# Segment sums of x added by accumulating DMAs in float32 instead of by matmuls, in a fused scan and memory-attention kernel

## The chip, the cores and the metric

The kernel runs on one core of one Trainium2 chip. The metric is device time in microseconds (us); lower is better. Each kernel was run several times. The engines are called as in the profile: PE is TensorE (matmuls), PEld its weight loads, DVE is VectorE, ACT is ScalarE, POOL is GpSimd, SP is SyncE.

## The reference, cut to what matters

The program computes two independent layers of the same width and joins their outputs. Layer A is a complex linear recurrence (a scan) over 2048 positions. Layer B is attention over 64 segments of 32 rows with an 8-row memory that is handed from segment to segment.

```python
# layer A
Bu = einsum('bld,pd->blp', x, B_bar)
for t in range(2048):
    h = Lam_bar * h + Bu[:, t, :]          # complex, 1024 states
y = 2 * einsum('blp,dp->bld', hseq, C).real + x * Dskip
# layer B, for each of 64 segments
h = concat([mem, xs])                      # 8 + 32 rows
o = softmax(mask(q k^T * scale)) v ; o = o @ Wo
mem = o[:, :8]                             # the next segment's memory
```

The kernel does not run layer B's 64 steps one after the other. It guesses every segment's memory from the mean of the segment's rows (the sum of 32 rows of x over L = 40, then through Wv and Wo), computes everything from the guess, and checks the guess at the end against a tolerance of 2^-8. If the check fails, a slow loop runs. The change concerns the segment sums that this guess starts from.

## The kernel before

In the "scan phase", about 35 to 347 us, TensorE works through a fixed list of steps. There are 32 scan blocks (block n = 4*pc + q) with 16 matmuls into the PSUM tile psU, and 32 "v groups" with four times 8 matmuls into psP. VectorE runs the scan of each block, and ScalarE copies both the scan's result (a_g) and the v results (b_vst) out of the way, in program order. This is part of a block:

```python
def stage1(self, pc, tb):
    u = k.ps("U", (128, 2, TB))                        # psU, 2 buffers
    ...  # 16 matmuls u <- a_xT, a_bt
    V.tensor_tensor(pr[:], u..., view(t3, ...), ALU.mult)   # the "large multiply"
    V.tensor_tensor(w, w, pr[:, :, 1, :], ALU.add)
    for j in range(2):
        V.tensor_tensor_scan(w[:, j, :], rb, w[:, j, :], carry, ALU.mult, ALU.add)
        S.activation(g[:, j, :], w[:, j, :], ACT.Copy)      # a_g, ScalarE
    ...  # the carry for the next block: five small instructions on GpSimd
    V.tensor_tensor(n[:], g..., view(r3, ...), ALU.mult)
    V.tensor_tensor(h[:], n[:, :, 0, :], n[:, :, 1, :], ALU.add)  # a_h
    k.SP.dma_start(self.hs[tb][:, pc, :, :], h[:])
```

The sums are made on TensorE, in eight groups of 16 matmuls that have only four columns each, one group ahead of each of the blocks 3 to 10:

```python
def sum_x(self, tmp):
    ...
    p = k.ps("R")
    for t in range(TT):                                # two t for each block
        xr = xrs.pop(t)                                # 128 rows of x, bf16
        for c in range(KC):
            o = c * NSEG + 4 * t
            k.PE.matmul(p[:, o:o + 4], xr[:, c * 128:(c + 1) * 128], k.ind[:], start=True, stop=True)
        load(t + 4)
        yield
    ...  # VectorE: xbar = p / L, with the memory's own mean in segment 0
```

The means are used by "og" groups (32 matmuls of 64 columns, psR<-b_xbar,b_wv), the first of which stood behind v group (3,3). Instructions that the program passes to `keep_in_program_order` are pinned within their engine; the others may be moved by the scheduler of the build.

Of the kernel before, what the change touches and what calls it, by code (L numbers as in the profile page):

```python
# [8 lines left out]
FP32 = mybir.dt.float32  # L9
BF16 = mybir.dt.bfloat16  # L10
I32 = mybir.dt.int32
ACT = mybir.ActivationFunctionType
ALU = mybir.AluOpType
# [26 lines left out]
EW = E + 8  # L40
# [53 lines left out]
def consts(k):  # L94
    nc, V, G = k.nc, k.V, k.G
    c = k.cst
    k.ident = c.tile([128, 128], BF16, name="ident")
    G.memset(k.ident[:], 1.0)
    G.affine_select(out=k.ident[:], in_=k.ident[:], compare_op=ALU.is_equal, fill=0.0, base=0,
                    pattern=[[-1, 128]], channel_multiplier=1)  # L100
    k.ones = c.tile([128, 1], BF16, name="ones")
    V.memset(k.ones[:], 1.0)
    k.hpb = c.tile([128, 1], FP32, name="hpb")
    k.hpe = c.tile([128, 1], FP32, name="hpe")
    V.memset(k.hpb[:], HALF_PI)
    k.S.activation(k.hpe[:], k.hpb[:], ACT.Exp)
    k.ind = c.tile([128, 4], BF16, name="ind")
    G.memset(k.ind[:], 0.0)
    for j in range(4):
        G.memset(k.ind[32 * j:32 * j + 32, j:j + 1], 1.0)  # L110


def masks(k):
# [223 lines left out]
class PartB:  # L337
# [34 lines left out]
        k.V.tensor_copy(self.memT[:, :, 0:NMX + 1], self.m0T[:])  # L372
        k.V.memset(self.accR[:], 0.0)

    def fill(self, tmp):
        k = self.k
        z = tmp.tile([32, 4 * EW], BF16, name="b_xr", bufs=4)
        k.V.memset(z[:], 0.0)
        for hb in range(HB):
            k.SP.dma_start(self.vx[hb][64 + NMX:GX, :], z[0:GX - 64 - NMX, :])  # L380
            k.SP.dma_start(self.vx[hb][T + 32:NSLOT, :], z[0:32, :])
        for q in range(4):
            k.SP.dma_start(self.tn[q][NM:NR, 0:4 * EW], z[0:NR - NM, :])
            k.SP.dma_start(self.tn[q][NM:NR, 1024 - 4 * EW:1024], z[0:NR - NM, :])
# [13 lines left out]
        return [(64 + 1536, 1536, 384), (0, XMAIN, 64), (T - 64, T - 64, 64)]  # L398

    def load_x0(self, tmp, i):  # L400
        self.x0.append(tmp.tile([128, D], BF16, name="b_xr", bufs=4))
        self.k.SP.dma_start(self.x0[i][:], self.x[0][64 + 128 * i:192 + 128 * i, :])

    def turn_x0(self, i):

        k = self.k
        pt = k.ps("U", (128, 2, KC, 128), BF16)[:, 0, :, :]
        for c in range(KC):
            k.PE.transpose(pt[:, c, :], self.x0[i][:, c * 128:(c + 1) * 128], k.ident[:])
        k.copy("vs"[i % 2], self.xe[:, :, 128 * i:128 * i + 128], pt)  # L410

    def sum_x(self, tmp):

        k = self.k
        xrs = {}

        def load(t):
            if t < TT:
                xrs[t] = tmp.tile([128, D], BF16, name="b_xr", bufs=4)
                k.SP.dma_start(xrs[t][:], self.x[0][t * 128:(t + 1) * 128, :])  # L420
        for t in range(4):
            load(t)
        yield
        p = k.ps("R")
        for t in range(TT):
            xr = xrs.pop(t)
            for c in range(KC):
                o = c * NSEG + 4 * t
                k.PE.matmul(p[:, o:o + 4], xr[:, c * 128:(c + 1) * 128], k.ind[:], start=True, stop=True)
            load(t + 4)  # L430
            yield
        pv = p[:].rearrange("p (c s) -> p c s", c=KC)
        ms = tmp.tile([128, KC], FP32, name="b_ms", bufs=1)
        k.V.tensor_reduce(ms[:], self.m0T[:], AX.X, ALU.add)
        k.V.tensor_scalar(self.xbar[:], pv, 1.0 / L, None, ALU.mult)
        k.V.tensor_tensor(ms[:], ms[:], pv[:, :, 0], ALU.add)
        k.V.tensor_scalar(self.xbar[:, :, 0], ms[:], 1.0 / L, None, ALU.mult)
        yield
# [536 lines left out]
def kernel_main(tc, A_x, A_Lre, A_Lim, A_Bre, A_Bim, A_Cre, A_Cim, A_logdt, A_Dskip, B_x, B_mem0, B_Wq, B_Wk, B_Wv, B_Wo, out,  # L975
                force=False, dbg=None):
    with ExitStack() as ctx:
        k = K(tc, ctx)
        k.dbg = dbg
        nc = k.nc  # L980
        a = PartA(k, A_x, A_Lre, A_Lim, A_Bre, A_Bim, A_Cre, A_Cim, A_logdt, A_Dskip, out)
        b = PartB(k, B_x, B_mem0, B_Wq, B_Wk, B_Wv, B_Wo, out)
# [11 lines left out]
        with pool("p1x", "right") as p1x, pool("p1", "right", 1) as p1:  # L994
            a.tab = a.tmp = a.wp = a.btp = p1
            k.pin |= {"PE", "SP"}
            warm(k, p1)
            w0 = b.wl.tile([128, KC, 512], BF16, name="b_wv", bufs=2)
            b.load_wv_part(w0, 0, 0, 128, nc.scalar)
            b.x0 = []  # L1000
            for i in range(4):
                b.load_x0(p1, i)
                if i in (1, 2):
                    b.load_wv_part(w0, 0, 128 * i, (256, 512)[i - 1])
            wv = {0: w0, 1: b.load_wv(1)}
            consts(k)
            a.load_params(p1)
            b.load_m0(p1)
            b.stage_init()
            order = steps()  # L1010
            b.v_x(0, 0, wv[0])
            b.load_x(1)
            a.load_b(0)
            a.xT = p1x.tile([128, KC, T], BF16, name="a_xT", bufs=1)
            a.load_x(0)
            a.params(p1, p1)
            b.init(p1)
            a.tables(0)
            loads = [[(b, 2)], [(a, 1), (a, 2)], [(b, 3), (a, 3)]]
            sx = b.sum_x(p1)  # L1020
            tabs = {0: a.tabs}
            bts = {0: a.bt}
            for kind, pc, q in order[1:]:
                if loads and kind == "v":
                    for o, n in loads.pop(0):
                        o.load_x(n)
                if kind == "v":
                    b.v_x(pc, q, wv[pc])
                    if q == 3:
                        if pc >= 3:  # L1030
                            b.og(pc, wv[pc])
                        n = (pc + 2) if pc + 2 < PC else (2, 0)[pc + 2 - PC]
                        wv[n] = b.load_wv(n)
                    continue
                a.tabs, a.bt = tabs[pc], bts[pc]
                n = 4 * pc + q
                if q == 2 and pc + 1 < PC:
                    a.load_b(pc + 1)
                    bts[pc + 1], a.bt = a.bt, bts[pc]
                if pc >= 4 and q == 1:  # L1040
                    a.load_c(pc - 4)
                if n == 1:
                    next(sx)
                if n >= 3:
                    for _ in range(2):
                        next(sx, None)
                a.stage1(pc, q)
                if q == 2 and pc + 1 < PC:
                    a.tables(pc + 1)
                    tabs[pc + 1] = a.tabs  # L1050
                if n == 12:
                    masks(k)
                    check_consts(k)
                if n == 14:
                    b.fill(p1)
            k.pin.remove("PE")
        psu.close()
        k.psx = ctx.enter_context(tc.tile_pool(name="pss", bufs=1, space=PSUM, reuse_waits="tile"))
# [5 lines left out]
        with pool("p2h", "right") as p2h, pool("p2", "right") as p2:  # L1064
# [5 lines left out]
            for i, _ in enumerate(s2):  # L1070
                if i in (1, 4, 7):
                    n = (2, 0, 1)[(i - 1) // 3]
# [148 lines left out]
```

## Time and profile before

| | before |
|---|---|
| time, median of the runs beside the change | 1247.47 us (1247.30 to 1248.05) |
| span of the profiled run | 1245.6 us |
| PE busy | 1234.4 us, 99% |
| chain that ended last | 98% PE |
| waits of PE of any size, 30 to 345 us | none |

The first lines are from the page of the kernel before: part 1, the busy time of each engine, and part 4, the chain of work that ended last, by engine.

```profile
PE 1234.4 (99%) x8270; PEld 662.3 (53%) x8342; DVE 668.0 (54%) x1250; ACT 263.5 (21%) x631; POOL 275.8 (22%) x407
...
PE 98%; DMA 1%; issue 0%; ACT 0%; POOL 0%; DVE 0%; SPq 0%; ACTq 0%
```

TensorE never stops. VectorE's 54% is an average over the whole program. The next lines are two of the 30 us windows of the same kernel, with the busy time of each engine, the granted clock, the DMA share and GB/s.

```profile
core 0: us, PE busy (x) PEld busy (x) DVE busy (x) ACT busy (x) POOL busy (x), PEclk, DMA share, GB/s
120.00:150.00 30.00, 29.84 (x166) 14.04 (x168) 26.56 (x28) 11.32 (x20) 9.96 (x15) 1.00 0.55 162
150.00:180.00 30.00, 29.84 (x166) 14.11 (x167) 29.05 (x27) 13.44 (x23) 7.97 (x10) 1.00 0.26 85
```

In the second window VectorE is busy for 29.05 of 30 us. The next lines are the timeline of PE in the kernel before; the columns are start, duration, engine, line, operation, tiles, shape and count.

```profile
60.13 7.07 PE L64 MATMUL psP<-b_wv,b_xe 128*128 128x512 bf16 x31
67.04 0.54 PE L64 MATMUL psR<-ind,b_xr 128*128 128x4 bf16 x16
67.44 3.61 PE L64 MATMUL psU<-a_xT,a_bt 128*128 128x512 bf16 x16
70.89 7.07 PE L64 MATMUL psP<-b_wv,b_xe 128*128 128x512 bf16 x31
```

One group of sum matmuls occupies 67.04 to 67.44, which is 0.40 us. Starts are to be subtracted, since the printed durations overlap. A scan block takes 3.45 us (70.89 less 67.44), so one 512-column matmul costs 0.216 us.

### The profile page before, as it was taken

How to read it: one execution, taken by the hardware profiler on the slowest of the kernel's cores; microseconds unless marked ns; L12 is line 12 of the kernel's file. 1: busy time of each engine (PE TensorE's matmuls, PEld its weight loads, DVE VectorE, ACT ScalarE, POOL GpSimd, SP SyncE). 2: the span in 40 equal slices, each digit the busy share in tenths (PEclk: the TensorE clock that was granted, in tenths of full speed). 3: DMA queues.
4: the chain of work that ended last, by engine and by line, in shares of the span. 5: the costliest groups of instructions: out<-in, count | busy, mean ns of one | idle time of the engine just before them, and what ended most of it. 6: DMA issues, size and time to landing. Idle time of an engine off the chain costs nothing.

```text
span 1245.6 us, 20120 instructions
## 1 busy us (share of the span) xinstructions
PE 1234.4 (99%) x8270; PEld 662.3 (53%) x8342; DVE 668.0 (54%) x1250; ACT 263.5 (21%) x631; POOL 275.8 (22%) x407
## 2 busy tenths in 40 slices
PE   9999999999999999999999999999999999999998
PEld 5444444444455555556666656555665554446444
DVE  4688899998711124666666666666666641001000
ACT  5344444443310000211112111111211110000000
POOL 4111331212332321322222222222222220000000
PEclk9999999999999999999999999999999999999999
DMA  9965444554898834664454544545473289407000
GB/s 245 272 192 148 131 132 128 144 156 107 241 323 247 251 116 95 192 167 123 95 144 108 144 108 114 138 92 133 96 155 95 61 223 220 110 18 153 17 17 27
DMA packets 316022, 176.83 MB, mean 142 GB/s; under 512 B 138650, under 2 KB 301326, under 8 KB 315926
## 3 DMA queue, kind: packets, MB, share of 16 engines
q1 hardware_dynamic: 293830, 147.95, 48.1%
q10 hardware_dynamic: 21072, 24.38, 5.9%
q0 software_dynamic: 1024, 3.17, 0.7%
q8 instruction: 66, 1.08, 0.4%
q14 instruction: 30, 0.25, 0.1%
HBM read 89.14 MB, written 53.17 MB: 114 GB/s over the span
## 4 chain that ended last, share of the span: by engine, by line
PE 98%; DMA 1%; issue 0%; ACT 0%; POOL 0%; DVE 0%; SPq 0%; ACTq 0%
PE psP L64 82%; PE psU L64 9%; PE psS L64 3%; PE psO L64 2%; PE psR L64 2%; DMA wo<-in_B_Wo_dram 1%; DMA b_xr<-in_B_x_dram 0%; ACT b_xe L89 0%; POOL b_m L644 0%; DVE b_ost L91 0%; SPq L64 0%; ACT b_e L641 0%; ACTq L89 0%
## 5 line engine op out<-in xcount | busy, mean ns | idle before, releaser
L64 PE MATMUL psP<-b_xe,b_wq 128*128 128x480 bf16 (+1 forms) x1280 | 247.7, 343 | 0.1
L64 PE MATMUL psP<-b_xe,b_wk 128*128 128x480 bf16 (+1 forms) x1280 | 247.7, 343 | 0.0
L64 PE MATMUL psP<-b_wv,b_xe 128*128 128x512 bf16 (+2 forms) x1033 | 223.4, 372 | 1.0 <-ACT b_xe L89 0.2
L644 POOL TENSOR_TENSOR b_m<-b_e,maskB 99x396 bf16<-99x396 bf16 x160 | 139.8, 874 | 334.0 <-ACT b_e L641 334.0
L641 ACT ACTIVATE b_e<-psS 99x396 bf16<-99x396 f32 x176 | 88.2, 501 | 532.2 <-PE psS L64 527.9
L64 PEld LDWEIGHTS <-b_wk 128*128 128x128 bf16 x1280 | 119.4, 98 | 94.2
L64 PEld LDWEIGHTS <-b_wq 128*128 128x128 bf16 x1280 | 118.7, 98 | 87.7
L64 PEld LDWEIGHTS <-b_xe 128*128 128x128 bf16 x1056 | 101.8, 98 | 119.1 <-ACT b_xe L89 0.4
L91 DVE CAST b_k<-psP 128x480 bf16<-128x480 f32 (+1 forms) x192 | 97.5, 529 | 101.1 <-PE psP L64 101.1
L91 DVE CAST b_q<-psP 128x480 bf16<-128x480 f32 (+1 forms) x192 | 97.5, 529 | 93.0 <-PE psP L64 91.4
L64 PEld LDWEIGHTS <-b_ol 128*128 128x128 bf16 x864 | 84.3, 98 | 94.4
L64 PE MATMUL psU<-a_xT,a_bt 128*128 128x512 bf16 x493 | 113.9, 379 | 1.1
L64 PE MATMUL psP<-t,a_hl 128*128 128x512 bf16 x496 | 112.1, 379 | 0.8
L91 DVE CAST b_ost<-psP 128x512 bf16<-128x512 f32 (+1 forms) x17 | 11.5, 676 | 183.4 <-PE psP L64 182.4
L64 PE MATMUL psP<-wo,b_ol 128*128 128x512 bf16 (+1 forms) x440 | 91.9, 364 | 0.4
L64 PE MATMUL psP<-t,b_ol 128*128 128x512 bf16 x408 | 91.7, 379 | 0.4
L280 POOL TENSOR_SCALAR a_tt<-a_pr,a_tabf 128x1 f32<-128x1 f32 x48 | 34.1, 709 | 243.5 <-DVE a_pr L275 243.5
L89 ACT ACTIVATE b_vst<-psP 128x512 bf16<-128x512 f32 x126 | 72.0, 589 | 71.0 <-PE psP L64 65.0
L661 DVE TENSOR_TENSOR b_ob<-psO,b_accR 99x384 bf16<-99x384 f32 x160 | 85.9, 553 | 2.0
L267 DVE TENSOR_TENSOR a_pr<-psU,a_tabf 128x2048 f32<-128x2048 f32 x32 | 73.0, 2282 | 15.7 <-PE psU L64 14.0
L64 PEld LDWEIGHTS <-a_bt 128*128 128x128 bf16 x512 | 49.2, 98 | 57.6
L64 PEld LDWEIGHTS <-a_hl 128*128 128x128 bf16 x512 | 49.1, 98 | 56.7
(200 smaller groups left out, 963.8 us busy)
## 6 DMA issues: line engine op xcount, KB each, us to landing
b_v<-b_vx SPq DMA_DIRECT2D x16, 1122.0 KB
b_wv<-in_B_Wv_dram SPq DMA_DIRECT2D x16, 1024.0 KB
b_on<-b_ob SPq DMA_DIRECT2D x15, 960.0 KB
b_vx<-b_vst ACTq DMA_DIRECT2D x24, 544.0 KB
a_hs<-a_h SPq DMA_DIRECT2D x32, 256.0 KB
b_wog<-in_B_Wo_dram SPq DMA_DIRECT2D x4, 2048.0 KB
b_wq<-in_B_Wq_dram SPq DMA_DIRECT2D x16, 512.0 KB
b_wk<-in_B_Wk_dram SPq DMA_DIRECT2D x16, 512.0 KB
```

Source lines behind the costliest of these rows:

```text
L64: r = f(*a, **kw)
L89: self.S.activation(out, in_, ACT.Copy)
L91: self.V.tensor_copy(out, in_)
L267: V.tensor_tensor(pr[:], u[:].unsqueeze(1).to_broadcast([128, 2, 2, TB]), view(t3, [[TB + 1, 2], [TB + 1, 2], [1, TB]]), ALU.mult)
L280: G.tensor_scalar(tt[:, j:j + 1], w[:, j, TB - 1:TB], t3[:, 1, TB:TB + 1], None, ALU.mult)
L641: k.S.activation(e[:], s[0:GW, :, :, 0:GW], ACT.Exp, scale=float(E) ** -0.5, accum_out=self.accE[0:GW, i:i + 1])
L644: k.G.tensor_tensor(m[0:GW, 0:4 * GP].rearrange("p (a b q) -> p a b q", a=2, b=2)[:, :, :, 0:GW], e[:], mask[0:GW, :, :].unsqueeze(2).to_b ...
L661: V.tensor_tensor(self.ob[:, b0:b0 + n, :], o[0:GW, 0:n, 0:E], r.unsqueeze(2).to_broadcast([GW, n, E]), ALU.mult)
```

## The change

The change wants the 3.2 us of sum matmuls off TensorE. Sixteen DMAs read x so that partition p gets row 16*p + j in the j-th DMA; the first two write float32 accumulators and fourteen add into them. VectorE adds the two accumulators (called the join below), ScalarE makes a bf16 high half, VectorE subtracts to get a low half, and 16 matmuls of 64 columns finish the sums, since now only two partitions belong to one segment. As the means are ready later, the first og group and one weight load move four blocks later.

```diff
-    def sum_x(self, tmp):
-        ...
-                xrs[t] = tmp.tile([128, D], BF16, name="b_xr", bufs=4)
-                k.SP.dma_start(xrs[t][:], self.x[0][t * 128:(t + 1) * 128, :])
-        ...
-                k.PE.matmul(p[:, o:o + 4], xr[:, c * 128:(c + 1) * 128], k.ind[:], start=True, stop=True)
+    def sum_x(self, tmp, ct):
+        k = self.k; G = k.G
+        acc = tmp.tile([128, 2, D], FP32, name="b_xr", bufs=1)
+        rows = self.x[0].rearrange("(p j) d -> p j d", j=16)
+        for j in range(16):
+            op = {"accum_op": ALU.add} if j > 1 else {}
+            k.tc.keep_in_program_order(G.dma_start(acc[:, j % 2, :], rows[:, j, :], **op))
+            if j % 2:
+                yield
+        s = acc[:, 0, :]
+        hl = ct[:, 0, 0:2, :]
+        k.tc.keep_in_program_order(k.V.tensor_tensor(s, s, acc[:, 1, :], ALU.add))
+        yield
+        k.tc.keep_in_program_order(k.S.activation(hl[:, 0, :], s, ACT.Copy))
+        yield
+        k.tc.keep_in_program_order(k.V.tensor_tensor(hl[:, 1, :], s, hl[:, 0, :], ALU.subtract))
+        yield
         yield
         p = k.ps("R")
+        for c in range(KC):
+            for i in range(2):
+                k.PE.matmul(p[:, c * NSEG:(c + 1) * NSEG], hl[:, i, c * 128:(c + 1) * 128], k.ind[:], start=(i == 0), stop=(i == 1))
@@ main loop
-                        if pc >= 3:
+                        if pc > 3:
                             b.og(pc, wv[pc])
                         n = (pc + 2) if pc + 2 < PC else (2, 0)[pc + 2 - PC]
-                        wv[n] = b.load_wv(n)
+                        if pc != 3:
+                            wv[n] = b.load_wv(n)
 ... (load_c of block n stands here, unchanged)
-                if n == 1:
-                    next(sx)
                 if n >= 3:
-                    for _ in range(2):
-                        next(sx, None)
+                    next(sx, None)
+                if n == 17:
+                    b.og(3, wv[3])
+                    wv[5] = b.load_wv(5)
                 a.stage1(pc, q)
```

Cut from the diff: `ind` becomes a 128x64 indicator built by two selects, the first four x tiles become slices of one tile, and a zero tile is taken from C's space.

More of the change, by code (lines that the diff above doesn't have):

```diff
@@ L106, in consts @@
     k.S.activation(k.hpe[:], k.hpb[:], ACT.Exp)
-    k.ind = c.tile([128, 4], BF16, name="ind")
-    G.memset(k.ind[:], 0.0)
-    for j in range(4):
-        G.memset(k.ind[32 * j:32 * j + 32, j:j + 1], 1.0)
+    k.ind = c.tile([128, NSEG], BF16, name="ind")
+    G.memset(k.ind[:], 1.0)
+    for base, m in ((0, 1), (1, -1)):
+        G.affine_select(out=k.ind[:], in_=k.ind[:], compare_op=ALU.is_ge, fill=0.0, base=base,
+                        pattern=[[-2 * m, NSEG]], channel_multiplier=m)
 def masks(k):
@@ L373, in init, with fill @@
         k.V.memset(self.accR[:], 0.0)
-    def fill(self, tmp):
+    def fill(self, ct):
         k = self.k
-        z = tmp.tile([32, 4 * EW], BF16, name="b_xr", bufs=4)
-        k.V.memset(z[:], 0.0)
+        z = ct[0:32, 0, 2, 0:4 * EW]
+        k.V.memset(z, 0.0)
         for hb in range(HB):
@@ L400, in load_x0 @@
     def load_x0(self, tmp, i):
-        self.x0.append(tmp.tile([128, D], BF16, name="b_xr", bufs=4))
-        self.k.SP.dma_start(self.x0[i][:], self.x[0][64 + 128 * i:192 + 128 * i, :])
+        if i == 0:
+            self.x0 = tmp.tile([128, 4, D], BF16, name="b_xr", bufs=1)
+        self.k.SP.dma_start(self.x0[:, i, :], self.x[0][64 + 128 * i:192 + 128 * i, :])
     def turn_x0(self, i):
@@ L408, in turn_x0 @@
         for c in range(KC):
-            k.PE.transpose(pt[:, c, :], self.x0[i][:, c * 128:(c + 1) * 128], k.ident[:])
+            k.PE.transpose(pt[:, c, :], self.x0[:, i, c * 128:(c + 1) * 128], k.ident[:])
         k.copy("vs"[i % 2], self.xe[:, :, 128 * i:128 * i + 128], pt)
-    def sum_x(self, tmp):
-        k = self.k
-        xrs = {}
-        def load(t):
-            if t < TT:
-                xrs[t] = tmp.tile([128, D], BF16, name="b_xr", bufs=4)
-                k.SP.dma_start(xrs[t][:], self.x[0][t * 128:(t + 1) * 128, :])
-        for t in range(4):
-            load(t)
+    def sum_x(self, tmp, ct):
[15 more added lines that the diff above has]
+        yield
         yield
         p = k.ps("R")
-        for t in range(TT):
-            xr = xrs.pop(t)
-            for c in range(KC):
-                o = c * NSEG + 4 * t
-                k.PE.matmul(p[:, o:o + 4], xr[:, c * 128:(c + 1) * 128], k.ind[:], start=True, stop=True)
-            load(t + 4)
-            yield
+        for c in range(KC):
+            for i in range(2):
+                k.PE.matmul(p[:, c * NSEG:(c + 1) * NSEG], hl[:, i, c * 128:(c + 1) * 128], k.ind[:], start=(i == 0), stop=(i == 1))
         pv = p[:].rearrange("p (c s) -> p c s", c=KC)
@@ L999, in kernel_main @@
             b.load_wv_part(w0, 0, 0, 128, nc.scalar)
-            b.x0 = []
             for i in range(4):
@@ L1019, in kernel_main @@
             loads = [[(b, 2)], [(a, 1), (a, 2)], [(b, 3), (a, 3)]]
-            sx = b.sum_x(p1)
+            sx = b.sum_x(p1, a.CT)
             tabs = {0: a.tabs}
@@ L1054, in kernel_main @@
                 if n == 14:
-                    b.fill(p1)
+                    b.fill(a.CT)
             k.pin.remove("PE")
```

## The prediction

> **What bounds the kernel.** TensorE: the page's first part has PE busy 1234.4 of 1245.6 us, and the chain of waits is 98% PE. The windows of 30 us between 30 and 330 us (scan phase, the only one the change touches) show PE at 29.8 of 30, DVE at 25 to 29. So only TensorE time counts, unless something new makes TensorE wait. VectorE is nearly co-critical there: from 150 to 287 us its large multiply (a_pr<-psU) waits for TensorE only twice, 1.8 us in all.
>
> **What is removed.** 128 segment-sum matmuls (psR<-ind,b_xr) in eight groups of 16, each before a scan block. In the timeline of PE a group starts at 67.04 and the next block's matmuls at 67.44: 0.40 us a group, all eight alike, 3.24 us in all. (The durations printed, 164 ns each, overlap and mislead.)
>
> **What is added.** 16 matmuls with 64 columns: the og group, same width, takes 0.93 us for 32 (170.39 to 171.32), so 0.47 us. Net TensorE gain 2.8 us. VectorE gets two fp32 128x1024 operations, 1.22 us each (as a_pr<-a_pr 128x1024 f32), ScalarE one copy of about 1.1 us. The xbar work and the first og copy only move.
>
> **The accumulating DMAs.** Sixteen 256 KB reads leave the SP queue for GpSimd's; 14 add into fp32. [...]the built order shows GpSimd waiting so, two chains of eight, in front of the scan carries. A plain 256 KB load from GpSimd lands in 5.8 us (DMA view); I estimate 6 to 9 us with the add. Carries are about 10 us apart and the fours fall in 20 us gaps, so I expect carries not to be late. The last pair is issued near 135 us, lands near 143; the VectorE join comes near 145 us. That margin is thin.
>
> **VectorE lag.** TensorE comes 2.8 us earlier, VectorE about 1 us earlier by block 16, so VectorE's lag grows by about 2 us. PSUM psU has two buffers; the smallest slack I find is 5.5 us: no stall.
>
> **The deferral.** og(3) and the wv load for pc 5 move from 170 to 195 us. In SP's order that load now follows the C transposes, which follow a_hs of block 16. Before, these issued at 208.4 to 214.4; now about 1 us earlier, so wv is issued near 213.4 and[...] lands near 219. TensorE wants it at 220.6-2.8 = 217.8. I expect a wait of about 1 us (0 to 3) on b_wv, which is new.
>
> **Sum.** 1247.49 - 3.24 + 0.47 + 1.0 + 0.3 (small ScalarE/psP waits) = 1246.0 us. Range 1243.8 to 1250.0. Chances: faster by over 2% 0.01, within 2% 0.96, slower by over 2% 0.03.
>
> **What would show it.** PE timeline: no gaps of 0.40 us before blocks 3 to 10, one of about 0.5 us before block 15, og (0.93 us) before block 17. Waits: PE or PEld waiting for DMA b_wv near 218 us, 0 to 3 us. GpSimd's timeline: carries start when VectorE's scan ends, not later. No VectorE wait for DMA b_xr at the join over 1 us. PE busy falls by about 3 us.
>
> **What would make it wrong.** Accumulating DMAs landing in over 10 us: GpSimd blocks, carries come late, VectorE, then ScalarE and psP evacuation, then TensorE stall, some us each block.[...] Or wv landing early: then 1244.7.

Three passages that no trace of this case shows are cut from this text, and the cuts are marked. The waits of GpSimd are waits for an earlier DMA into the same accumulator. The forecast's sum came to 1247.49 - 3.24 + 0.47 + 1.0 + 0.3 = 1246.0 us. Its 1.0 us is the wait on b_wv, 219 less 217.8 us, put at about 1; this term was the author's estimate. The trace after the change shows 1.04 us for ScalarE's copy, which the text puts at about 1.1.

## More of the kernel before

A v group takes four of psP's three rotating banks in turn, so its fourth set of 8 matmuls needs ScalarE's copy of an earlier one:

```python
    for i in range(4):
        p = k.ps("P")[:]                               # psP, 3 buffers
        self.v_mm(p, w, 4 * q + i)                     # 8 matmuls
        k.copy("s", st[:, i, :, 0:E], p...)            # b_vst, ScalarE
```

## The result, and the profile after

The changed kernel took 1258.87 us (1256.14, 1258.69, 1259.05 and 1259.61), against 1247.47 us before: 0.9% slower, and outside the predicted range. Ratios in this document are the mean time of one kernel's fast runs over the mean of the other's fast runs of the same rounds, so they are not quite the ratios of the medians quoted. Here the ratio is 1.0087, with a 95% interval of 1.0069 to 1.0104. The profiled run is the 1256.14 one (span 1254.4 us, 8.8 us more than before), and what follows explains these 8.8 us.

The page of the changed kernel, the same two parts as before:

```profile
PE 1234.1 (98%) x8159; PEld 659.2 (53%) x8230; DVE 670.0 (53%) x1252; ACT 264.6 (21%) x632; POOL 290.7 (23%) x421
...
PE 93%; DVE 3%; DMA 3%; issue 1%; POOL 0%; ACT 0%; SPq 0%; DVEq 0%; POOLq 0%
```

PE's busy time fell by only 0.3 us where 2.8 was expected, and its share of the chain fell from 98% to 93%, with DVE and DMA taking 3% each. The same two windows after the change:

```profile
120.00:150.00 30.00, 27.10 (x125) 12.22 (x125) 19.90 (x18) 8.31 (x15) 10.81 (x14) 1.00 0.75 211
150.00:180.00 30.00, 23.98 (x100) 10.41 (x102) 28.99 (x29) 13.68 (x23) 9.10 (x10) 0.89 0.18 66
```

VectorE lost 6.7 us in the first window; TensorE lost 2.7 us there and 5.9 us in the second, where its granted clock was also below 1. Every other window from 30 to 330 us has PE at 29.8 us. So the loss happens once. The timeline of DVE after the change shows where it starts; the bracket gives the idle time just before an instruction and what ended it. (Line numbers differ a little between kernels.)

```profile
136.79 0.69 DVE L288 TENSOR_TENSOR a_h<-a_n 128x1024 bf16<-128x1024 bf16 x1
146.64 1.23 DVE L427 TENSOR_TENSOR b_xr<-b_xr 128x1024 f32<-128x1024 f32 x1 [9.16 <-DMA b_xr<-in_B_x_dram]
147.78 2.28 DVE L268 TENSOR_TENSOR a_pr<-psU,a_tabf 128x2048 f32<-128x2048 f32 x1
```

VectorE finished block 9 at 137.5 us and came to the join, which stands ahead of block 10's large multiply (147.78) in its order. It waited 9.16 us for the last accumulating DMA, although psU for block 10 was full. The timeline of PE after the change shows the consequence:

```profile
143.59 3.62 PE L64 MATMUL psU<-a_xT,a_bt 128*128 128x512 bf16 x16
150.12 3.61 PE L64 MATMUL psU<-a_xT,a_bt 128*128 128x512 bf16 x16 [2.91 <-DVE a_pr L268]
153.57 5.34 PE L64 MATMUL psP<-b_wv,b_xe 128*128 128x512 bf16 x23
164.71 3.57 PE L64 MATMUL psP<-b_wv,b_xe 128*128 128x512 bf16 x8 [5.79 <-ACT b_vst L89]
168.07 4.01 PE L64 MATMUL psU<-a_xT,a_bt 128*128 128x512 bf16 x16
```

TensorE waits twice: 2.91 us for a psU buffer that VectorE had not read, and 5.79 us for a psP bank that ScalarE had not emptied. Then it is slow. The 8 matmuls from 164.71 take 3.36 us (to 168.07), 0.42 us each instead of 0.216. One-microsecond windows of the changed kernel, for PE alone, show why; PEclk, the number right after the count, is the granted clock as a share of full speed.

```profile
core 0: us, PE busy (x), PEclk, DMA share, GB/s
165.00:166.00 1.00, 1.00 (x4) 0.50 0.00 0
166.00:167.00 1.00, 1.00 (x4) 0.50 0.00 0
167.00:168.00 1.00, 1.00 (x3) 0.50 0.00 0
168.00:169.00 1.00, 1.00 (x4) 0.57 0.52 205
```

The clock was exactly halved until about 169 us, for the first 4.15 us of work after the wait. The clock records of this trace have it at 0.50 from 162.03 to 168.86 us, 6.83 us in all: it fell 3.11 us after TensorE went idle at 158.92, while the 5.79 us wait still lasted, and came back 4.15 us after the wait had ended. The wait of 2.91 us cost no clock; the records stay at 1.00 through it and after it, up to 162.03 us. Busy time is therefore useless as a measure here: PE is "busy" with the same work for longer.

The books close on TensorE. Block 11 began 2.62 us earlier than before (143.59 against 146.21 us), which is the saving of the eight sum groups, 3.24 us, less a start about 0.6 us later. Block 13, the first after the waits, began at 168.07 against 160.03 us, 8.04 us later. So 10.66 us were lost between: 2.91 and 5.79 us of waits, 1.63 us of half clock (3.36 us for 8 matmuls instead of 1.73), and 0.33 us of ends of matmuls (the last matmul before each wait is drawn with its full 0.379 us, 0.163 us more than the usual step of 0.216). The remaining slow matmuls cost 0.40 us more (3.85 us for the block at 168.07 instead of 3.45), and the 16 new matmuls 0.47 us (189.18 to 189.65). The sum, 8.04 + 0.40 + 0.47 = 8.91 us, is the span's 8.8 us within 0.1.

The chain of waits of the changed kernel, in order of time (start, duration, what), leads from GpSimd to TensorE:

```profile
129.25 0.62 POOL b_xr L422
129.87 9.42 DMA b_xr<-in_B_x_dram
...
139.58 6.98 DMA b_xr<-in_B_x_dram
...
146.64 1.23 DVE b_xr L427
147.87 2.21 DVE a_pr L268
...
163.13 1.04 ACT t L429
164.17 0.49 ACT b_vst L89
```

GpSimd began to issue the seventh pair of DMAs at 129.25, right after a carry. By the chain, the pair had landed at 139.29, after 9.42 us; only then was the last DMA on the same bytes issued (139.58), and it took 6.98 us. That GpSimd waits so was read from the built order in the prediction, and the trace shows it: GpSimd's DMA issues waited 11.2 us in all, six times, for earlier DMAs into b_xr. Whether the sums would come out wrong without these waits was not tested. Note the last two lines also: ScalarE's high-half copy (t, 1.04 us) ran ahead of the b_vst copy that TensorE needed. What it alone adds to the wait was not tested.

### The profile page after: what moved, and what is told of

Same layout as the page of the kernel before. It is cut to its first block, busy times and chain, and to the rows that moved or that the text cites. A ratio compares the mean times of both kernels' runs of the same rounds, so it can differ in the third digit from the quotient of the medians.

```text
span 1254.4 us, 19885 instructions
## 1 busy us (share of the span) xinstructions
PE 1234.1 (98%) x8159; PEld 659.2 (53%) x8230; DVE 670.0 (53%) x1252; ACT 264.6 (21%) x632; POOL 290.7 (23%) x421
## 2 busy tenths in 40 slices
DMA packets 316020, 181.00 MB, mean 144 GB/s; under 512 B 138650, under 2 KB 301326, under 8 KB 315926
## 4 chain that ended last, share of the span: by engine, by line
PE 93%; DVE 3%; DMA 3%; issue 1%; POOL 0%; ACT 0%; SPq 0%; DVEq 0%; POOLq 0%
PE psP L64 79%; PE psU L64 7%; PE psS L64 3%; PE psO L64 2%; PE psR L64 1%; DMA b_xr<-in_B_x_dram 1%; DVE a_pr L268 1%; DVE a_pr L276 1%; DMA wo<-in_B_Wo_dram 1%; DMA b_wv<-in_B_Wv_dram 1%; DVE a_pr L271 0%; DVE a_n L287 0%; POOL a_tt L281 0%; POOL a_nx L282 0%; SPq L64 0%
```

## The experiments

A wait of 9 us is a cause that can be read from the trace. But two questions can not be read. Would the change have paid without the wait? And if not, is VectorE's added work to blame, or the traffic, or the deferral? My theory from here on was that in the scan phase VectorE and TensorE are in balance, so that work added to VectorE comes back as waits of TensorE. Rivals were the DMA traffic, GpSimd's blocking and the deferred load.

One measure is used throughout. The "shift" is the start of VectorE's large multiply of a block in the experiment's profile less the same in the kernel before; that of block 31, the last, lies within 0.7 us of the difference of the two spans in every run that did not fall back, and within 0.1 us in the changed kernel, e1, d9, d4, n1 and h6. The kernel before took 1247.24 to 1247.36 us on the chips of these runs. Many of the times that I expected were missed: e1, e2, f1, f2, h2, h7 and h8 came out 0.3 to 2.8 us slower than the range of my theory, d9 and n1v 0.7 and 0.3 us faster. The traces therefore decide more than the times.

| run | us, median (range) | ratio to before | shift at block 31, us | TensorE waits in the scan phase, us |
|---|---|---|---|---|
| after | 1258.87 (1256.14 to 1259.61) | 1.0087 | +8.90 | 2.91, 5.79 |
| a2_after_again | 1257.33 (1256.37 to 1259.98) | 1.0088 | +9.41 | 3.0, 5.8 |
| e1_join_later | 1248.59 (1248.11 to 1249.28) | 1.0009 | +1.92 | 2.2 |
| e2_dmas_earlier | 1249.81 (1247.19 to 1250.13) | 1.0014 | +2.78 | 2.0 in two, 2.3 |
| d9_vector_held_9us | 1253.27 (1252.76 to 1254.15) | 1.0049 | +5.60 | 1.2, 3.6 in three |
| d4_vector_held_4us | 1249.97 (1249.71 to 1250.15) | 1.0021 | +2.47 | 2.3 in two |
| f1_gpsimd_join | 1247.89 (1247.61 to 1248.42) | 1.0005 | +0.91 | 2.4 |
| f2_gpsimd_join_wv_first | 1248.12 (1246.98 to 1249.18) | 1.0008 | -0.03 | 1.8 |
| g1_deferral_alone | 1247.60 (1247.36 to 1248.19) | 1.0004 | -0.36 | none |
| x1_one_x0_tile | 1247.16 (1246.87 to 1247.27) | 0.9998 | -0.25 | none |
| n1_no_sums | 1244.27 (1244.04 to 1244.52) | 0.9976 | -3.28 | none |
| n1v_no_sums_vector_2us | 1246.38 (1246.08 to 1246.84) | 0.9992 | -0.68 | 1.9 |
| h1_start_restored | 1247.14 (1246.91 to 1247.35) | 0.9999 | -0.04 | 1.8 |
| h2_og_copies_on_scalar | 1246.87 (1246.39 to 1249.98) | 1.0004 | -0.54 | 1.6 |
| h3_no_low_half | 8335 (fell back) | | -1.60 | 0.6 |
| h4_no_low_og_scalar | 8323 (fell back) | | -2.03 | none |
| h6_gpsimd_quarters | 1245.55 (1245.26 to 1246.29) | 0.9985 | -0.99 | 0.5 |
| h7_float32_matmuls | 1247.30 (1247.07 to 1247.71) | 0.9999 | +0.25 | none |
| h8_float32_og_scalar | 1247.23 (1246.74 to 1248.87) | 1.0000 | +0.54 | none |

### The wait itself: e1_join_later and e2_dmas_earlier

The first moves the join one block later in the program. The second starts the DMAs two blocks earlier and leaves the join at the same call.

```diff
 # e1_join_later, against the changed kernel
         hl = ct[:, 0, 0:2, :]
+        yield
         k.tc.keep_in_program_order(k.V.tensor_tensor(s, s, acc[:, 1, :], ALU.add))
 ...
         k.tc.keep_in_program_order(k.V.tensor_tensor(hl[:, 1, :], s, hl[:, 0, :], ALU.subtract))
         yield
-        yield
```

> The changed kernel with only the VectorE join moved one scan block on in the program (its pin now hangs on the last add of block 11, not on a table operation that floats early); the accumulating DMAs, GpSimd's waits, the deferred og and wv load are as they were. Theory A (the loss is VectorE held in order at the join by the last accumulating DMAs): no wait of VectorE over 0.5 us at the join, no TensorE wait on psU or psP, clock 1.000, 1244.5 to 1246 us, and the spread between runs back under 1 us. Rival B (GpSimd waiting on the DMAs delays the scan carries, or the DMA traffic itself slows things): the loss stays, 1253 to 1259 us.

The join's wait is gone, the time falls by 10 us to 1248.59, and so the wait and what followed from it are shown as the cause of nearly the whole loss. But the kernel is still not faster than before; the ratio is 1.0009 with an interval of 0.9996 to 1.0023. TensorE's saving was there: at block 11 the shift is -2.62 us. By block 15 it was +0.06, and at block 31 it was +1.92. In the profile of PE one new wait appears:

```profile
204.37 2.56 PE L64 MATMUL psP<-b_wv,b_xe 128*128 128x512 bf16 x8 [2.22 <-ACT b_vst L89]
206.72 4.67 PE L64 MATMUL psU<-a_xT,a_bt 128*128 128x512 bf16 x16
```

The 8 and the 16 matmuls take 2.35 and 4.51 us instead of 1.73 and 3.45. One-microsecond windows of the same run and engine show the clock again at half until about 208.9 us:

```profile
206.00:207.00 1.00, 1.00 (x4) 0.50 0.00 0
207.00:208.00 1.00, 1.00 (x3) 0.50 0.00 0
208.00:209.00 1.00, 1.00 (x4) 0.58 0.00 0
```

So a wait of only 2.2 us was followed by half clock here, and cost 1.7 us on top. The window from 205 to 206 us has a mean clock of 0.72 and the one from 208 to 209 has 0.58, so the half clock lasted from about 205.4 to 208.8 us, 3.4 us, and began about 1.1 us after the wait had ended at 204.37. This is the profile of the slowest run (1249.28 us, mean clock 0.998). Three of e1's five runs have a mean clock of 1.000 and took 1248.11 to 1248.59 us, so they probably had no half clock; none of them was profiled. The place of the wait is telling. In the kernel before, the same v group runs there with no wait, but with almost no room. These are the timelines of ACT and of PE in the kernel before:

```profile
202.95 0.63 ACT L276 ACTIVATE a_g<-a_pr 128x512 bf16<-128x512 f32 x1 [0.49 <-DVE a_pr L275]
203.48 1.55 ACT L89 ACTIVATE b_vst<-psP 128x512 bf16<-128x512 f32 x3
...
198.95 6.85 PE L64 MATMUL psP<-b_wv,b_xe 128*128 128x512 bf16 x31
```

ScalarE waits for VectorE's scan, copies a_g, and only then starts on the three waiting psP banks. The first of these copies ends at about 204.0 us (a third of 1.55 after 203.48), and TensorE needs the bank at 198.95 + 3 x 1.727 = 204.13. The slack was about 0.1 us. Any microsecond by which TensorE gains on VectorE before this point is lost here.

```diff
 # e2_dmas_earlier, against the changed kernel
         hl = ct[:, 0, 0:2, :]
+        yield
+        yield
         k.tc.keep_in_program_order(k.V.tensor_tensor(s, s, acc[:, 1, :], ALU.add))
 ...
-                if n >= 3:
+                if n >= 1:
                     next(sx, None)
```

> The changed kernel with the accumulating DMAs started two blocks earlier; the scheduler then also puts the join one block earlier in VectorE's order, still about one block after the last pair is issued. Theory A: the last pair lands near 124 us, the join is reached near 126, wait 0 to 2 us, TensorE not held, 1244.5 to 1247 us. Rival B (more DMA traffic in the busy first 60 us and GpSimd waits as before): no better than 1253 us.

In the built order the join moved ahead of block 9, and the shift there is +1.42 us where the changed kernel has -1.15. With TensorE no longer held at 150 us, the wait that I had predicted for the deferred weight load did appear, in the timeline of PE:

```profile
223.38 6.87 PE L64 MATMUL psP<-b_wv,b_xe 128*128 128x512 bf16 x31 [2.27 <-DMA b_wv<-in_B_Wv_dram]
```

Three of its four runs took 1249.6 to 1250.13 us and one took 1247.19. The profiled run is one of the slow ones, so this spread is not explained here.

### VectorE held on purpose: d9_vector_held_9us and d4_vector_held_4us

Here the kernel before gets nothing but a memset on VectorE ahead of block 10, into space that C needs only later. No DMA and no matmul changes.

```diff
 # against the kernel before; 613 for d9, 307 for d4
+                if n == 10:
+                    z = a.CT[:].rearrange("p a c d -> p (a c) d")[:, :, 0:613]
+                    k.tc.keep_in_program_order(k.V.memset(z, 0.0))
                 a.stage1(pc, q)
```

> The kernel before (sums on TensorE, no accumulating DMA) with one VectorE memset of unused memory of about 9.2 us put where the join stands in the changed kernel: after block 9, before block 10's large multiply. Theory A: holding VectorE for 9 us is enough; TensorE waits about 3 us on psU and 5 us on psP, then some us at a lower clock: 1254 to 1258 us. Rival B: without the DMAs there is no loss beyond 2 us: 1247.5 to 1249.5 us.

> The same with a memset of about 4.6 us. Theory A with the slack I read from the trace of before (5.5 us on psU): TensorE hardly waits, 1247.5 to 1249 us, so the loss is not proportional to the hold. If the slack is smaller than read: 1250 to 1253 us.

In d9 the multiply of block 10 came 9.13 us later and the end 5.60 us later; in d4 it was 4.03 and 2.47. So holding VectorE makes TensorE wait (1.2 us on psU and 3.6 us on psP in d9) without any new DMA. But of the 9 us only about 60% arrives, so the hold alone is not the whole loss of the changed kernel. One difference is known: no wait in d9 exceeded 1.8 us and its mean clock was 1.0, so the 2.0 us of half clock are missing. What makes the remaining 1.3 us at block 31 was not tested. TensorE's waits differ by more, 8.7 us against 4.8; in the changed kernel TensorE had come 2.6 us ahead before it was held. d4 also contradicts the slack of 5.5 us on psU that I had read: after a hold of 4 us TensorE waited 2.3 us, on psP.

### The joining work on another engine: f1_gpsimd_join and f2_gpsimd_join_wv_first

```diff
 # f1_gpsimd_join, against e1_join_later
-        k.tc.keep_in_program_order(k.V.tensor_tensor(s, s, acc[:, 1, :], ALU.add))
+        k.tc.keep_in_program_order(G.tensor_tensor(s, s, acc[:, 1, :], ALU.add))
 ...
-        k.tc.keep_in_program_order(k.V.tensor_tensor(hl[:, 1, :], s, hl[:, 0, :], ALU.subtract))
+        k.tc.keep_in_program_order(G.tensor_tensor(hl[:, 1, :], s, hl[:, 0, :], ALU.subtract))
```

> The late-join kernel with the join and the subtraction moved from VectorE to GpSimd. Theory A2 (what is left of the loss in the late-join kernel is VectorE's lag: 2.4 us more work and TensorE 2.8 us earlier, which reaches TensorE through ScalarE's in-order queue and psP near 201 us): the psP wait of 2.2 us near 201 and the lower clock after it go, and in its place a wait of 1 to 2.5 us on b_wv near 219 us appears, as in the kernel with the earlier DMAs; 1246 to 1247.5 us. Rival C (GpSimd's operations block VectorE's two-input operations for as long, 2.1 us each): psP wait stays, 1248 to 1250 us.

```diff
 # f2_gpsimd_join_wv_first, against f1_gpsimd_join
-                if pc >= 4 and q == 1:
-                    a.load_c(pc - 4)
                 if n >= 3:
                     next(sx, None)
                 if n == 17:
                     b.og(3, wv[3])
                     wv[5] = b.load_wv(5)
+                if pc >= 4 and q == 1:
+                    a.load_c(pc - 4)
```

> The same, and the deferred wv load issued ahead of the C transposes in SP's queue. If the b_wv wait comes from standing behind the transposes it goes: 1244.7 to 1246 us, faster than both kernels by about 2 us. If not: as the kernel before it.

Rival C was a guess; the traces of h1 (below) and h2 show such a hold, of one add, by 2.0 us beside a GpSimd subtraction of 2.12 us. Both kernels come out level with the kernel before. The shift at block 31 went from +1.92 (e1) to +0.91 (f1) to -0.03 (f2), but the 2.7 us of TensorE are still not seen. The 0.9 us between f1 and f2 are not all due to the weight load. Where b_wv is needed, f1 lost only about 0.2 us on TensorE (3.69 us from the scan block at 217.81 to the v group behind it, against 3.45 us in f2). Another 0.6 us arose earlier: VectorE's half-sum at 149.80 us took 1.86 us in f1, against 1.22 us in f2 (at 149.74), which fits a later join on GpSimd beside it, but the cause was not tested. In f2 the shift is -2.45 at block 13 and -0.82 at block 14, so the loss falls into a single block, the one in which GpSimd does the subtraction. f2 has no wait on b_wv. f1's wait of 2.43 us on psP was not followed by half clock (its next 8 matmuls took 1.72 us, and the granted clock was 1.00 in every one-microsecond window from 204 to 208 us), while e1's wait of 2.22 us was. So the length of a wait alone did not decide here whether it cost the clock; what did is not shown. f2's profiled run is one of its three at a mean clock of 1.000 (1246.98 to 1248.12 us); the two at 0.998 took 1248.83 and 1249.18 us.

### Parts of the change alone: g1_deferral_alone and x1_one_x0_tile

```diff
 # g1_deferral_alone, against the kernel before
-                        if pc >= 3:
+                        if pc > 3:
                             b.og(pc, wv[pc])
 ...
+                if n == 17:
+                    b.og(3, wv[3])
+                    wv[5] = b.load_wv(5)
 # x1_one_x0_tile, against the kernel before
-        self.x0.append(tmp.tile([128, D], BF16, name="b_xr", bufs=4))
+        if i == 0:
+            self.x0 = tmp.tile([128, 4, D], BF16, name="b_xr", bufs=1)
```

> The kernel before with only the og of pc 3 and the wv load for pc 5 deferred to block 17. My prediction's step (wv needed at 220.6 us, landing about 220 to 221 in this kernel where VectorE and so the transposes are at their old times): a wait on b_wv of 0 to 1.5 us, 1247.3 to 1249 us. Rival: no wait, 1247.4.

> The kernel before with its four x tiles made slices of one tile, as in the changed kernel, and nothing else. The three kernels with the change start their first scan block on TensorE at 36.55 us, those without at 35.85 to 35.96. If the single tile is the cause: 36.5 and 1248.0 us. If it is the changed GpSimd start (indicator, parameter loads 0.25 us earlier): 35.9 and 1247.4 us.

Neither moves the time (1.0004 and 0.9998). The deferral alone makes no wait on b_wv. With the single tile, the first scan block started at 35.71 us on TensorE, so this does not explain the later start of the changed kernel and its variants (36.4 to 36.8 us, against 35.6 to 36.2 for the kernel before and its variants; h7 and h8, further below, began at 35.9 and 36.2). In eight of the eleven late profiles the timeline of TensorE shows a wait of 0.30 to 0.67 us for a load of b_wv at 9.6 to 10.0 us (0.55 us in the changed kernel), which that of the kernel before does not; e2 and f2, late as well, show none there, so this is not the whole cause.

### The ceiling, and the price of VectorE's work: n1_no_sums and n1v_no_sums_vector_2us

The first takes the sum matmuls out of the kernel before altogether (one matmul stays, so that the tile is written) and forces the result of the check, as its means are meaningless. It is no usable kernel; it shows what TensorE can gain at most. The second adds a memset of about 2.3 us on VectorE ahead of block 13.

```diff
 # n1_no_sums, against the kernel before
-            for c in range(KC):
-                o = c * NSEG + 4 * t
-                k.PE.matmul(p[:, o:o + 4], xr[:, c * 128:(c + 1) * 128], k.ind[:], start=True, stop=True)
+            if t == 0:
+                k.PE.matmul(p[:], xr[:, 0:128], xr[:, 0:512], start=True, stop=True)
 ...
+        k.V.memset(b.flag[:], 0)
 # n1v_no_sums_vector_2us, on top of it
+                if n == 13:
+                    z = a.CT[:].rearrange("p a c d -> p (a c) d")[:, :, 0:165]
+                    k.tc.keep_in_program_order(k.V.memset(z, 0.0))
```

> The kernel before without its 128 segment-sum matmuls (one 512-column matmul left so that the PSUM bank is written; the guess is then wrong on purpose and the check's flag is set to 0 so that the fall-back does not run; the loads and all VectorE work stay). This measures what TensorE's saving is worth when nothing is added: both theories say nearly all of 3.0 us, 1244.3 to 1245.2 us, because before block 11 VectorE was waiting for TensorE and follows it; VectorE's block 12 should then start about 2.4 us earlier than in the kernel before.

> The same with one VectorE memset of about 2.5 us before block 13, the size of the join and the subtraction. Theory P (TensorE and VectorE are in balance in the scan phase, so VectorE's added work costs what it takes): the gain is gone again, 1246.7 to 1247.6 us, with a TensorE wait on psP behind ScalarE near 204 us. Rival T (work on VectorE is free while TensorE is the busiest engine, as my prediction had it): 1244.3 to 1245.2 us.

Without the sums the kernel takes 1244.27 us, a ratio of 0.9976 (0.9961 to 0.9992), and the shift is -3.28 us to the end with no wait at all (0.29 us of it an earlier start). TensorE's saving is real, and it lasts as long as VectorE gets nothing in return. With the memset the shift is -0.68 at the end and the time 1246.38. These are the memset in the timeline of DVE and the wait in that of PE:

```profile
164.54 2.26 DVE L1048 MEMSET t<- 128x2640 bf16 x1 [0.50 <-issue]
...
203.45 1.89 PE L64 MATMUL psP<-b_wv,b_xe 128*128 128x512 bf16 x8 [1.94 <-ACT b_vst L89]
```

About 2.8 us more on VectorE (2.26 and the 0.50 ahead of it) at 164 us became 1.94 us of waiting on TensorE at 203 us, at the very place with the zero slack, and 2.1 us of time (0.5 us of the difference between the two profiles is the start of the first block, 35.67 and 36.17 us). The join and the subtraction of the changed kernel are 2 x 1.22 us. This run is the step that the prediction lacked.

### Taking the holds away: h1, h2 and h6

h1_start_restored is f2 with GpSimd's first instructions as before; h2_og_copies_on_scalar also moves the copies of the og results from VectorE to ScalarE; h6_gpsimd_quarters also cuts GpSimd's join and subtraction into four pieces.

```diff
 # h1_start_restored: GpSimd first fills a small tile as it did; the code that builds the
 # 128x64 indicator moves to block 12 (in the built order it ran at 5.4 to 6.5 us)
-    G.memset(k.ind[:], 1.0)
+    k.pad = c.tile([128, 4], BF16, name="pad")
+    G.memset(k.pad[:], 0.0)   # and the four small memsets
 # h2_og_copies_on_scalar
-        k.copy("s" if late else "v", self.ogT[...], p[...])
+        k.copy("s", self.ogT[...], p[...])
 # h6_gpsimd_quarters; the join likewise
-        k.tc.keep_in_program_order(G.tensor_tensor(hl[:, 1, :], s, hl[:, 0, :], ALU.subtract))
+        for c in range(0, D, 256):
+            k.tc.keep_in_program_order(G.tensor_tensor(hl[:, 1, c:c + 256], s[:, c:c + 256], hl[:, 0, c:c + 256], ALU.subtract))
```

> The kernel with the join on GpSimd and the wv load first, with GpSimd's first instructions as in the kernel before (four small memsets of an unused tile) and the indicator built after them. If the changed GpSimd start is what makes TensorE begin its first scan block at 36.5 to 36.8 us: 35.6 to 36.0 us now. The total can gain 0.7 us at most: 1246.4 to 1248 us. If the first block stays at 36.5 or later, the cause is another.

> The same with the five og copies of the scan phase on ScalarE in place of VectorE (0.42 us each). Theory P: VectorE's block 31 comes up to 2 us earlier than in the kernel before and TensorE's saving shows: 1245 to 1246.5 us, the first version faster than both. If ScalarE's queue is the tighter one: no better than 1247.4 us.

h1 took 1247.14 us, and its first scan block still began late, at 36.70 us. The indicator was still built before the first block, only later, so h1 alone does not clear GpSimd's start work; but h7 and h8, further below, have the same start (with a float32 indicator) and were punctual. h1's trace gave the reason for f2's lost block. These are the timelines of DVE and of POOL in h1:

```profile
173.01 2.65 DVE L292 TENSOR_TENSOR a_h<-a_n 128x1024 bf16<-128x1024 bf16 x1
...
172.99 2.12 POOL L436 TENSOR_TENSOR t<-b_xr,t 128x1024 bf16<-128x1024 f32 x1
```

The a_h add takes 0.69 us elsewhere. It started 0.02 us after GpSimd's subtraction, and took 2.65 us. It ended 0.55 us after the subtraction did, nearly its usual length of 0.69 us. So work moved from VectorE to GpSimd still held VectorE for 2.0 us (2.65 less 0.69). GpSimd's join in the same run (147.27, 2.36 us) ran beside a large multiply with an input in PSUM, which took its normal 2.29 us.

> As h2_og_copies_on_scalar, but the GpSimd join and subtraction are each cut into four pieces of 128x256. My theory (VectorE and TensorE are in balance, so what VectorE waits or works shows up in TensorE): VectorE's half-sum at the subtraction is held at most about 0.7 us instead of 2 us more than its usual 0.69, so VectorE ends 1 to 1.5 us earlier than in h2 and the time is 1245.4 to 1246.6 us. Rival (the holding of VectorE by GpSimd is absorbed by slack): same as h2, 1246.7 to 1247.2.

In h6, with the subtraction in pieces, VectorE was held for less. These are the same two instructions in h6:

```profile
173.73 1.19 DVE L292 TENSOR_TENSOR a_h<-a_n 128x1024 bf16<-128x1024 bf16 x1
...
173.71 3.00 POOL L438 TENSOR_TENSOR t<-b_xr,t 128x256 bf16<-128x256 f32 x4
```

The hold is 0.5 us instead of 2.0. TensorE's wait on psP fell from 1.6 us (h2) to 0.5 us, the shift at the end is -0.99 us, and the time is 1245.55 us (1245.26 to 1246.29), with a ratio of 0.9985 and an interval of 0.9971 to 0.9998. This is the one correct version that beats both kernels, by about 1.8 us against the kernel before. Its profiled run is the slowest of its five. GpSimd pays with 3.00 us for the four pieces of the subtraction instead of 2.12. The join in pieces did not help: it took 4.69 us instead of 2.37 (h2), and the scan beside it 3.17 us instead of 2.46, so the shift at block 12 is -1.74 us where h2 has -2.75. It also began later (148.47 against 146.88 us), so cutting it up is not shown to be the cause.

### The low half left out: h3_no_low_half and h4_no_low_og_scalar

```diff
 # h3_no_low_half, against f2_gpsimd_join_wv_first; h4 is h3 with h2's copies
-        k.tc.keep_in_program_order(G.tensor_tensor(hl[:, 1, :], s, hl[:, 0, :], ALU.subtract))
 ...
-            for i in range(2):
-                k.PE.matmul(p[:, c * NSEG:(c + 1) * NSEG], hl[:, i, c * 128:(c + 1) * 128], k.ind[:], start=(i == 0), stop=(i == 1))
+            k.PE.matmul(p[:, c * NSEG:(c + 1) * NSEG], hl[:, 0, c * 128:(c + 1) * 128], k.ind[:], start=True, stop=True)
```

> The kernel with join on GpSimd and wv first, without the low half: no subtraction on any engine and 8 matmuls in place of 16, the sums rounded once to bf16 (the kernel's own check still runs, and falls back slowly if the guess is too far off). Theory P[...] (the GpSimd subtraction held VectorE's a_h add for 2.65 us in place of 0.69): VectorE's block 14 starts about 2.4 us earlier than in the kernel before, block 16 about 1.5 us earlier (the xbar work has moved behind block 14), 1245.4 to 1246.5 us. If VectorE's lead is lost elsewhere: 1247 or more.

> The same with the og copies on ScalarE, which takes 0.42 us off VectorE before block 17 and more later: theory P says 0.3 to 0.8 us faster than the same without this, 1244.8 to 1246 us; if ScalarE's queue binds, no faster.

Both give correct outputs, but only because the check of the guess failed and the slow loop ran: over 8300 us. So the low half is needed. Up to the end of the scan phase the traces can still be read. The shift is -1.60 us in h3 and -2.03 us in h4, and the wait on psP shrank to 0.6 us and to nothing. Taking GpSimd's subtraction away gave VectorE back what f2 had lost at block 14 (-2.41 there, against -0.82 in f2).

### The traffic or the joining: h7_float32_matmuls and h8_float32_og_scalar

These keep all sixteen accumulating DMAs and do no joining at all. The final 16 matmuls take both float32 accumulators directly as weights, with a float32 indicator.

```diff
 # h7_float32_matmuls, against h1_start_restored; h8 is h7 with h2's copies
-    k.ind = c.tile([128, NSEG], BF16, name="ind")
+    k.ind = c.tile([128, NSEG], FP32, name="ind")
 ...
-        (join, high-half copy and subtraction)
 ...
-                k.PE.matmul(..., hl[:, i, c * 128:(c + 1) * 128], k.ind[:], start=(i == 0), stop=(i == 1))
+                k.PE.matmul(..., acc[:, i, c * 128:(c + 1) * 128], k.ind[:], start=(i == 0), stop=(i == 1))
```

> No join, no ScalarE copy, no subtraction: 16 matmuls with float32 weights straight from the two accumulators and a float32 indicator of 64 columns, the rest as h1_start_restored. My theory: VectorE and ScalarE do none of the joining, so VectorE ends about 2.0 to 2.5 us before the kernel before (as n1 without sums did, 3.3); TensorE gains 3.24 us less the new matmuls[...], so 1.3 us less the start penalty of 0.6 us: 1246.0 to 1246.9 us. The guess check passes since float32 sums are at least as exact. Rival (the gap of the changed kernels is due to the DMA traffic of the accumulation and not to VectorE): 1247.4 or more, as f2.

> As h7_float32_matmuls, with the copies of the og results on ScalarE: VectorE gets less work again, about 1 us. My theory: as h7 or up to 0.5 us faster, as TensorE is now the one in front: 1245.7 to 1246.9 us, and no wait on psP over 1 us near block 16. Rival: as h7's rival, 1247.4 or more.

Both missed on time: 1247.30 and 1247.23 us, level with the kernel before, which is what the rival had put near. The traces decide against the rival all the same. In h7 the shift is -3.26 us at block 13 and -3.60 us at block 14, as good as in n1_no_sums, which has no accumulating DMA (-3.27 and -3.28), and TensorE waits nowhere. So the traffic costs nothing that shows. The gain goes later, in one step, and my size for that step was off. This is the timeline of PE in h7:

```profile
177.48 3.68 PE L64 MATMUL psR<-ind,b_xr 128*128 128x64 f32 x32
181.00 3.19 PE L64 MATMUL psU<-a_xT,a_bt 128*128 128x512 bf16 x13
```

The expectation's 1.3 us is the 3.24 us saved less a cost of the float32 matmuls that rested on no trace. They took 3.52 us (177.48 to 181.00), 7.5 times the 0.47 us of the bf16 ones in the changed kernel, and the profile counts 32 matmuls and 32 weight loads of 192 ns for 16 calls, against 16 and 16 of 98 ns in bf16. 3.24 us saved less 3.52 us paid is -0.28 us, and the shift at the end is +0.25. I had left out the weight loads. Whether they or the matmuls themselves set the 3.52 us was not tested.

### The changed kernel again: a2_after_again

The edit is none: this is the changed kernel. It was run at another time.

> The changed kernel unaltered, on the same chip as these. All theories: 1255 to 1260 us. Its profile says whether a run at 1258 to 1259 differs from the profiled one at 1256.1 by a longer hold at the join (over 9.2 us) or by a longer time at a lower TensorE clock.

The ratio is 1.0088, the join's wait 9.25 us, and TensorE's waits 3.0 and 5.8 us, so the loss repeats. Its runs spread again, from 1256.37 to 1259.98 us. The slower runs have a lower mean clock (0.995 to 0.996 against 0.997), which would fit a longer stretch at half clock. Another 3.4 us at half clock, as in e1, would lower the mean clock by 0.0014 and cost up to 1.7 us (an estimate from the length of e1's half clock and the span), but none of these runs was profiled, so this stays an argument.

## Why the prediction was wrong, point by point

- **What bounds the kernel: right in part.** TensorE was the bottleneck, and I noted that VectorE was "nearly co-critical". I then costed VectorE's new work as if it were free.
- **The saving on TensorE: right.** 3.24 less 0.47 us; e1's block 11 was 2.6 us earlier although it started 0.6 us later, and n1 showed 3.28 us, 0.29 of it an earlier start.
- **The landing of the DMAs: right in the main.** I estimated 6 to 9 us; the trace has 4.6, 6.4 and 9.4 us as minimum, median and maximum of the sixteen, two of them plain and fourteen accumulating, and each took GpSimd 0.56 to 1.21 us to issue (median 0.90). The carries were not late either.
- **"The VectorE join comes near 145 us": wrong, and the costliest step.** I read "about the time of block 11" from the loop. In the built order the join stands right behind block 9's a_h, so VectorE reached it at 137.5 us, a block earlier, and stood there for 9.16 us. The DMAs, too, landed later than the 143 us that I gave them, at 146.6, as the last one waited for the 9.42 us of the one before. I had called the margin thin, but listed its failure with no cost and kept the upper end of the range at 1250. Why the scheduler set the join so early I only read from the code: the join is pinned behind the VectorE instruction traced before it, a table instruction that itself runs early. This was not tested; that one more `yield` moves the join away from the wait was (e1).
- **"The smallest slack I find is 5.5 us: no stall": wrong.** I looked at psU alone. The binding slack was on psP, about 0.1 us at 204 us, by way of ScalarE, whose in-order queue puts VectorE's a_g ahead of TensorE's b_vst. n1v shows the price: 2.8 us on VectorE made 2.1 us of time. With the join's wait removed, e1's profile shows this second error, and the half clock after its wait, in place of the predicted gain.
- **"A wait of about 1 us (0 to 3) on b_wv": not seen after the change, real without the stall.** The changed kernel has no such wait, as TensorE was 9 us late by then. e2 had 2.27 us at 223 us. In f1 a delay of about 0.2 us was left, in f2, which asks for the weights ahead of the C transposes, none; e2 with the weights first was not run.
- **Missing from the prediction:** the half clock after a wait (2.0 us in the changed kernel, 1.7 us in e1) and the start of the scan phase about 0.6 us later. The cause of the latter is open; x1 speaks against the single tile, and h7 and h8, which started on time, against GpSimd's start work.

## What to carry to other kernels

When one engine is at 99%, find the second engine's busy share in the window that the change touches, and follow every buffer that both feed, through the in-order engine between them, before calling added work free. An instruction that waits on a DMA belongs in an engine's built order behind the moment of landing with a margin of several microseconds (here the last one landed 3.6 us later than I had put it, at 146.6 against 143 us), and that position has to be read from the built order, not from the loop. Moving work from VectorE to GpSimd gave back only a part here (e1 1248.59 us, h1 1247.14): GpSimd's subtraction held VectorE's next add for 2.0 us. Look at which VectorE instruction runs beside the moved one: in h1 a large multiply with an input in PSUM was not held (2.29 us beside the join), and in h6 a subtraction cut into quarters held the add for only 0.5 us. After a wait of TensorE, look at the granted clock too, run by run: 2.22 us in e1 were followed by half clock, 2.43 us in f1 and 2.91 us in the changed kernel were not.
